# Banded attention: score products in 64x64 quarters of the array, values products in row halves

## The chip, the cores and the metric

One NeuronCore of a Trainium2 chip (trn2). The time is the device time of one launch in microseconds; "span" is the length of the profiled execution, about 1.7 us shorter than the time of the same run. Runs come as fast or slow (slow: over 1.5% above the fastest of the same kernel); fast runs are compared with fast runs.

## The reference

Causal attention with ALiBi bias in a band of 128 keys (8 batches, 8 heads, 576 positions, head width 64), then a token mixer on the 8x576x512 result:

```python
scores = q @ k.T / 8 + slope[h] * -(i - j)          # where 0 <= i - j < 128, else -1e9
x = softmax(scores) @ v                              # heads side by side: [8, 576, 512]
W = (x @ w_q) @ (x @ w_k).T / 8
out = relu(W @ x) @ w_out
```

## The kernel before

Everything is laid out by hand: a list of operations, each with its engine, and one fixed order for each engine. Loads of q, k, v go through one DMA queue; GpSimd casts to fp16; TensorE (PE) transposes q and k; then come scores, exponentials (ScalarE, ACT), multiplication by a table of exp(bias) and mask (VectorE, DVE), values, normalisation, and the mixer. The parts that the change touches:

```python
# scores: key tiles of 128 keys; two heads at once, in the two row halves of the array (64 rows each)
for kb in ((0, 1), (2, 3, 4))[u]:
    for i in range(2):
        ps, r = bank(bk[i]), slice(64 * i, 64 * i + 64)
        ...                                            # a, w: 256, 192 or 64 query columns
        nc.tensor.matmul(ps[:, a : a + w], kk, qT[b % 2][r, c, P * kb : P * kb + w], start=True, stop=True)
nc.scalar.activation(out=pt[:, n % 4, :, 512 * u : 512 * u + 512], in_=..., func=AF.Exp, scale=SCALE)   # 128x1024
nc.vector.tensor_tensor(out=p_, in0=p_, in1=table[:, h0 : h0 + 3 : 2, :], op=ALU.mult)                  # 128x2048

# values: 18 products over all 128 rows for each pair of heads
for t in range(5):
    for i in range(2):
        o = px_of(bk)[:, i, 100 * t : 100 * t + 65]
        ...
        if t > 0:
            nc.tensor.matmul(o, p_[:, a : a + P], vt[b % 2][:, t - 1, hv], start=True, stop=False)
        ...
        nc.tensor.matmul(o, p_[:, a : a + P], vv, start=(t == 0), stop=True)
```

Each `matmul` becomes two PE instructions ("rows" from here on): a weight load and the product (2308 of each in the trace). A "step" below is the work of one pair of heads of one batch, 32 in all. Key tiles of 128 keys against 256 queries compute much that the band masks out; that is what the change goes after.

The softmax here doesn't subtract the row's maximum and nothing guards it: scores larger than these inputs give would overflow.

## Time and profile before

| | before |
|---|---|
| time, median of 3 | 151.97 us (151.51 to 154.68, the last a slow run) |
| span | 149.7 us |
| PE, DVE, ACT busy | 84%, 84%, 79% |
| PE rows in its program | 4618 (2308 weight loads and 2308 products in the trace) |

The waits of the kernel before (who waited for what: us in total, times, longest). "issue" is idle time for which the profile shows no cause:

```profile
PEld L159 <- issue: 21.9, 61, 1.0
...
PE bank L159 <- issue: 1.3, 2, 0.8
```

PEld's "issue" total of 21.9 us did not hold up the products: PE itself waited only 1.3 us for nothing visible.

Busy time by stretches of 30 us (stretch, length, then us busy and instructions of PE, PEld, DVE, ACT and POOL; the last columns are the granted clock, the DMA share and GB/s):

```profile
0.00:30.00 30.00, 20.02 (x392) 16.39 (x393) 23.10 (x43) 23.44 (x31) 11.94 (x20) 1.00 1.03 286
30.00:60.00 30.00, 25.01 (x540) 17.29 (x541) 27.80 (x44) 24.72 (x35) 18.14 (x23) 1.00 1.02 270
60.00:90.00 30.00, 27.94 (x528) 17.70 (x527) 27.67 (x47) 27.39 (x38) 15.67 (x18) 1.00 1.05 332
90.00:120.00 30.00, 28.19 (x526) 17.67 (x528) 28.42 (x46) 26.74 (x42) 12.55 (x18) 1.00 0.93 254
```

PE handles about 530 products in 30 us.

### The profile page before, as it was taken

What the parts mean: (1) busy time and instruction counts of PE and PEld (TensorE: products, weight loads), DVE (VectorE), ACT (ScalarE), POOL (GpSimd) and SP (SyncE); (2) the same over time, 40 slices, a digit from 0 to 9 for tenths busy, and PEclk for the clock granted to TensorE, in tenths of its full rate; (3) what the DMA queues carried; (4) which work ended last, traced back from release to release, by engine and by line L of the source; (5) the groups of instructions that cost most, each with busy time, mean ns of one, the idle gap of its engine ahead of it and who ended that gap; (6) DMA issues with size and microseconds to landing.
All of it is one profiled execution on the core that took longest, in us unless ns stands there. A gap on an engine that the chain in (4) does not pass through costs nothing.

```text
span 149.7 us, 5314 instructions
## 1 busy us (share of the span) xinstructions
PE 125.7 (84%) x2308; PEld 82.6 (55%) x2308; DVE 125.7 (84%) x212; ACT 118.5 (79%) x170; POOL 58.9 (39%) x78
## 2 busy tenths in 40 slices
PE   6567388676889979889989999999789999999870
PEld 6465167555756456547466566576544757555320
DVE  5749987979999998789999989999799989994700
ACT  6959937995889868997799999959889989741560
POOL 4064137354915767333845381364341710000000
PEclk9999999999999999999999999999999999999999
DMA  4999999999999999999999999799699896033075
GB/s 151 383 327 266 180 365 351 264 171 358 389 263 191 296 299 195 236 306 309 348 348 372 338 405 227 167 254 279 157 371 340 235 385 222 4 140 144 0 314 176
DMA packets 50775, 39.40 MB, mean 263 GB/s; under 512 B 39488, under 2 KB 39488, under 8 KB 50752
## 3 DMA queue, kind: packets, MB, share of 16 engines
q1 hardware_dynamic: 50752, 39.07, 88.7%
q8 instruction: 18, 0.29, 0.8%
q14 instruction: 5, 0.04, 0.1%
HBM read 29.62 MB, written 9.44 MB: 261 GB/s over the span
## 4 chain that ended last, share of the span: by engine, by line
PE 40%; DMA 16%; DVE 13%; ACT 12%; SPq 9%; POOL 4%; issue 2%; POOLq 0%; DVEq 0%
PE bank L159 40%; DMA ld<-in_q_dram 10%; SPq L159 9%; ACT pt L159 8%; DMA ld<-in_k_dram 6%; DVE pt L159 5%; POOL nat L159 2%; ACT qT L159 2%; DVE xT L159 2%; POOL vt L159 2%; DVE x L159 2%; ACT kT L159 1%; DVE kT L159 1%; DVE osb L159 1%; DVE rm L159 1%
## 5 line engine op out<-in xcount | busy, mean ns | idle before, releaser
L159 ACT ACTIVATE pt<-bank 128x1024 f16<-128x1024 f32 x64 | 62.7, 1036 | 9.3 <-PE bank L159 9.0
L159 POOL CAST nat<-ld 128x1152 f16<-128x1152 f32 x30 | 34.2, 1146 | 36.7 <-PE bank L159 10.6
L159 DVE TENSOR_TENSOR pt<-pt,table 128x2048 f16<-128x2048 f16 x32 | 41.0, 1293 | 2.1 <-ACT pt L159 2.0
L159 PE MATMUL bank<-wout_sb,rm 128*128 128x512 f16 x128 | 31.8, 380 | 0.0
L159 POOL CAST vt<-ldv 128x512 f16<-128x512 f32 (+1 forms) x35 | 20.8, 613 | 25.4 <-DVE pt L159 15.5
L159 PE MATMUL bank<-qT,kT 64*128 64x256 f16 (+2 forms) x320 | 25.4, 267 | 4.6 <-ACT qT L159 2.0
L159 PE MATMUL bank<-vt,pt 128*128 128x65 f16 x576 | 23.7, 200 | 4.6 <-ACT pt L159 3.1
L159 PEld LDWEIGHTS <-pt 128*128 128x128 f16 x576 | 21.4, 102 | 9.7 <-issue 2.6
L159 DVE TENSOR_TENSOR x<-bank,inv 128x640 f16<-128x640 f32 x32 | 25.8, 817 | 0.8
L159 PEld LDWEIGHTS <-kT 64*128 64x128 f16 x320 | 14.5, 99 | 11.5 <-issue 8.6
L159 ACT COPY osb<-bank 128x512 f32<-128x512 f32 x24 | 13.9, 606 | 7.1 <-PE bank L159 7.1
L159 PE MATMUL bank<-ident,nat 64*128 64x64 f16 x576 | 14.7, 199 | 5.6 <-POOL nat L159 2.8
L159 PEld LDWEIGHTS <-nat 64*128 64x128 f16 x576 | 12.2, 100 | 10.1 <-POOL nat L159 4.7
L159 PEld LDWEIGHTS <-rm 128*128 128x128 f16 x128 | 10.8, 98 | 12.6 <-issue 2.5
L159 ACT COPY qT<-bank 128x1152 f16<-128x1152 f16 x12 | 13.5, 1121 | 2.6 <-PE bank L159 2.6
L159 ACT ACTIVATE rm<-bank 128x512 f16<-128x512 f32 x21 | 12.7, 610 | 2.2 <-PE bank L159 2.2
L159 DVE COPY kT<-bank 128x1152 f16<-128x1152 f16 x8 | 10.8, 1354 | 3.2 <-PE bank L159 3.2
L159 DVE COPY xT<-bank 128x640 f16<-128x640 f16 (+1 forms) x32 | 12.5, 448 | 0.4 <-PE bank L159 0.4
L159 PE MATMUL bank<-x,wkn 128*64 128x512 f16 x80 | 10.1, 383 | 0.0
L159 PE MATMUL bank<-wqT,gm 64*128 64x256 f16 x64 | 8.4, 288 | 1.5 <-DVE wqT L159 0.6
L159 ACT COPY kT<-bank 128x1152 f16<-128x1152 f16 x8 | 9.1, 1138 | 0.5 <-PE bank L159 0.5
L159 DVE TENSOR_SCALAR rm<-bank 128x512 f16<-128x512 f32 x11 | 7.5, 684 | 2.3 <-PE bank L159 2.2
(45 smaller groups left out, 112.1 us busy)
## 6 DMA issues: line engine op xcount, KB each, us to landing
ld<-in_k_dram SPq DMA_DIRECT2D x16, 576.0 KB, 6.9
ld<-in_q_dram SPq DMA_DIRECT2D x16, 576.0 KB, 7.0
ldv<-in_v_dram SPq DMA_DIRECT2D x32, 256.0 KB, 7.1
out_dram<-osb SPq DMA_DIRECT2D x16, 512.0 KB, 5.2
ldv<-in_v_dram SPq DMA_DIRECT2D x8, 128.0 KB, 7.3
osb<-in_moe_w_out_dram SPq DMA_DIRECT2D x2, 512.0 KB, 7.1
out_dram<-osbt SPq DMA_DIRECT2D x8, 128.0 KB, 3.8
osbt<-in_moe_w_q_dram SPq DMA_DIRECT2D x1, 128.0 KB, 5.3
```

What stands on the lines that cost most here:

```text
L159: r = call(*a, **k)
```

## The change

Key tiles of 64 keys need only the two or three query tiles of 64 that the band reaches: 24 tiles of 64 columns for two heads, stacked on the partition halves, instead of 2048 columns for the pair. So the exponentials fall from 64 to 48 and the bias products from 2048 to 1536 columns. Score products shrink to 64x64 quarters, meant to run four at once; values are summed over 64 rows each, two heads at once in the row halves. (One product over 128 rows repeated every 30 ns before.) All operations were put in a new fixed order. The diff, cut to its core (table building, the v loads by pairs of heads, zero pads and the order list are cut):

```diff
-                    for kb in ((0, 1), (2, 3, 4))[u]:
+                    for s, t, n in units[u]:            # 14 (key tile, query tile, count) in three units
                         for i in range(2):
-                            nc.tensor.matmul(ps[:, a : a + w], kk, qT[b % 2][r, c, P * kb : P * kb + w], ...)
+                            for a in range(2):
+                                r, o = slice(64 * i, 64 * i + 64), slice(64 * a, 64 * a + 64)
+                                nc.tensor.matmul(
+                                    bank(bk[i])[o, w : w + 64 * n],
+                                    kT[b % 2][r, 2 * f + a, 64 * s : 64 * s + 64],
+                                    qT[b % 2][r, 2 * f + a, 64 * t : 64 * t + 64 * n],
+                                    start=True, stop=True)
...
-                nc.vector.tensor_tensor(out=p_, in0=p_, in1=table[:, h0 : h0 + 3 : 2, :],
+                    nc.vector.tensor_tensor(out=p_, in0=p_,
+                                            in1=table[:, n].rearrange("p (k w) -> p k w", k=6),
...
-                        (18 products over 128 rows)
+                    terms = [(j, column[j, j])]
+                    if t < 4:
+                        terms += [(j + 1, column[j + 1, j + 1] - 64)]
+                    if t > 0:
+                        terms += [(j - 1, column[j - 1, j]), (j - 2, column[j - 2, j])]
+                    for m, (s, a) in enumerate(terms):                      # 17 terms, 34 products
+                        for i in range(2):
+                            r = slice(64 * i, 64 * i + 64)
+                            nc.tensor.matmul(px_of(bk)[:, i, 100 * t : 100 * t + 65],
+                                             pt[r, c, a : a + P], vt[b % 2][r, s, c],
+                                             start=(m == 0), stop=(m == len(terms) - 1))
```

PE's program grows from 2308 products to 3396.

More of the change, by code (lines that the diff above doesn't have):

```diff
@@ L99 @@
 PLAN = """
-1G 6D 39S 4D 0G 35S 2D 7D 47S 3G 8P0 5D 43S 14P0 20A 65S 19A 11P0 23A 59S 18A 12P0 17A 61S 24A 25D
-21A 9P0 57S 22A 40A 15P0 53S 26D 13P0 51S 10P0 55S 36A 41P2 73S 42D2 69S 37P0 31S 38A0 48G 33S
-250P0 99S 49P2 251A0 44G 245P4 91S 50D2 243P6 77S 244A6 45P0 248P2 66G 46D0 246A4 249A2 67P6 247D
-260P0 255P4 261A0 258P2 62G 68D6 60A 253P0 259A2 58D 63P6 252D 64A6 256A4 262D 254A0 52D 54D 56A
-257D 85S 403P0 95S 406P2 79S 404D0 74G 405D0 265P4 81S 263P6 266A4 407D2 83S 408D2 411P0 70G 87S
@@ L105 @@
-264A6 414P4 412D0 413D0 117S 75P2 32G 71P6 29S 415D4 34G 409P0 416D4 72A6 27S 410D0 113S 417P4
-76A2 268P6 100G 418D4 270P0 269A6 280P2 267D 101P4 281A2 273P6 92G 102D4 274A6 531P2 78G 271A0
-532D2 278P6 93P4 86G 275P2 279A6 272D 535P0 94A4 96G 533P1 536D0 276A2 534D1 80G 537P4 539P0 277D
-111S 97P2 538A4 16P6 125S 98A2 82G 540D0 109S 84G 105S 282D 103S 427P0 419P2 107S 88G 428D0 121S
-295P4 420D2 429D0 422P6 296A4 143S 421D2 293P0 118G 89P4 294A0 423D6 424D6 430P2 90A4 431D2 30G
-541P0 425P6 432D2 542A0 283P4 426D6 433P2 284A4 28G 288P0 434D2 285P6 286A6 297D 290P4 547P2 289A0
@@ L111 @@
-543P6 287D 545P3 544A6 300P0 114G 546D3 291A4 119P6 548D2 549P3 120D6 301A0 126G 298P4 550A3 115P0
-292D 127P6 299A4 650P2 110G 128D6 116A0 645P3 106G 651A2 112G 137S 557P0 646D3 553P4 104G 643P2
-139S 554A4 558D0 133S 108G 644A2 135S 302D 435P0 131S 438P2 129S 122G 436D0 310P4 439D2 440D2
-648P6 147S 311A4 647S 437D0 303P2 144G 649A6 123P4 304A2 124D4 138G 145P0 446P6 146A0 308P2 140G
-447D6 448D6 443P4 309A2 555P0 444D4 441P6 134G 445D4 556A0 141P2 142A2 442D6 449P0 305P4 136G
-450D0 306A4 551P6 313P2 552D6 559P0 314A2 132G 307D 315P4 163S 318P6 316A4 320P2 157S 655P1 130G
@@ L117 @@
-560D0 151S 319A6 451P4 159S 321A2 663P0 148G 195S 452D4 453D4 177S 323P6 664A0 312D 325P2 165S
-149P4 656A1 161S 563P0 324A6 322D 169S 326A2 561P1 155S 317D 652S 454P6 564A0 462P2 150A4 164G
-455D6 562D1 653P0 463D2 152G 456D6 459P4 654A0 464D2 660P1 160G 657S 460D4 158G 461D4 173S 153P2
-661A1 328P6 189S 154D2 658P0 329A6 196G 203S 330P4 191S 659D0 565P6 333P2 331A4 199S 566D6 178G
-457P0 334A2 465P4 458D0 197P6 466D4 198A6 338P0 166G 571P2 572D2 340P4 339A0 573P6 327D 341A4
-575P7 162G 574D6 335P0 569P2 567P4 336A0 170G 577P6 568D4 570A2 576D7 156G 179P0 578D6 167P2 180A0
@@ L123 @@
-171P4 332D 467P6 168A2 666P0 337D 172A4 668P1 468D6 469D6 470P2 667A0 669A1 579P4 471D2 581P6
-472D2 174G 580A4 673P0 670S 582A6 662S 585P2 342D 175P4 185S 586A2 345P6 671P1 346A6 183S 190G
-674D0 181S 478P2 204G 176A4 672D1 187S 348P6 479D2 207S 480D2 475P0 349A6 192G 350P4 476D0 583P2
-477D0 351A4 473P6 200G 474D6 481P0 584A2 343P4 482D0 344A4 353P6 355P2 352D 587P0 356A2 683P1
-588D0 354A6 347D 678P0 684A1 186G 193P2 679A0 358P4 194D2 360P6 359A4 591P0 184G 361A6 357D 215S
-201P2 205P4 209S 202A2 589P1 182G 592D0 221S 681P6 590D1 206A4 217S 188G 211S 362D 491P0 682A6
@@ L129 @@
-233S 483P2 225S 492D0 486P4 484D2 216G 493D0 676P6 208G 487D4 485D2 686P7 210G 677A6 488D4 680S
-597P0 687A7 370P2 598D0 213S 494P4 371A2 222G 675S 593P6 495D4 373P0 594A6 496D4 241S 489P2 374A0
-229S 380P6 490D2 218G 497P4 665S 498D4 381A6 223P2 375P0 212G 224D2 365P4 237S 376A0 601P6 235S
-366A4 603P7 602D6 685S 377D 363P0 239S 599P2 368P4 364A0 605P6 600D2 226G 369A4 604D7 595P0 606D6
-234G 227P2 596A0 219P4 372D 378P6 220A4 696P0 214G 228D2 379A6 694P1 697A0 367D 613P4 607P2 609P6
-608A2 689P0 610A6 382D 507P2 614A4 691P6 690A0 242G 508D2 509D2 695A1 499P4 230G 692A6 611P0 500D4
@@ L135 @@
-383P2 501D4 612A0 693S 502P6 384A2 688S 238G 231P0 503D6 504D6 510P4 232A0 698S 709P2 236G 511D4
-512D4 385P0 505P6 386A0 400P4 506D6 701P3 401A4 710D2 240G 398P0 702D3 513P6 711S 399A0 393P4
-514D6 699P2 394A4 402D 615P3 700A2 395P0 616D3 388P4 703S 396A0 390P6 387D 617P2 389A4 619P3 618D2
-397D 391A6 515P0 706P2 620A3 516D0 392D 621P4 625P6 622A4 704P3 517D0 707A2 626D6 518P4 705A3
-627P0 519D4 708S 523P6 520D4 628A0 623P2 524D6 526P0 624A2 525D6 521P4 527D0 528D0 714P2 522D4
-529P0 715A2 712P3 530D0 629P2 713D3 631P0 630D2 716S 633P1 632D0 717P0 634A1 639P2 637P4 635P6
@@ L141 @@
-640A2 638D4 641P2 636D6 719P1 642A2 718D0 727P2 720D1 729P3 728A2 721S 724P2 730A3 731S 722P3
-725A2 732P2 723A3 726S 733A2 734S
+0G 6D 34S 30S 4D 1G 11P0 54S 2D 12P0 42S 14P0 5D 38S 3G 7P0 58S 46S 13P0 19A 9P0 18A 35G 17A 48S
+21D 8P0 16A 15P0 50S 36P2 31A 20D 10P0 52S 37A2 32P0 55G 62S 33A0 66S 56P2 78S 222P0 43G 57D2
+226P4 28S 223A0 224P6 26S 225A6 44P2 82S 39G 45D2 70S 227A4 40P0 59G 41A0 72S 228D 76S 230P0 234P2
+231A0 232P4 229D 60P6 74S 235A2 47G 61D6 22S 49G 350P0 233A4 24S 353P2 351D0 51G 86S 238P4 236D
@@ new lines @@
+240P6 90S 239A4 102S 53G 354D2 352D0 242P4 106S 237D 243A4 96S 358P0 63G 355D2 241A6 94S 359D0
+356P2 360D0 64P4 361P6 67G 100S 65A4 357D2 362D6 68P0 363D6 98S 79G 69A0 364P2 114S 365D2 29G 80P0
+110S 27G 250P4 81A0 245D 248P6 126S 478P2 244D 249A6 246P0 480P3 83G 479D2 251A4 482P2 481D3 247A0
+71G 84P4 483A2 253D 366P0 85A4 486P2 484P6 73G 367D0 368D0 485A6 120S 369P4 77G 487A2 490P0 370D4
+256P6 491A0 371D4 130S 377P2 257A6 488P0 252D 372P4 489A0 75G 373D4 254P6 258P0 255A6 23G 378D2
+379D2 374P4 259A0 375D4 25G 376D4 380P0 260D 597P2 87G 381D0 590P3 598A2 88P0 91G 591D3 492P2 89A0
@@ new lines @@
+493D2 92P4 261D 592P0 93A4 103G 593D0 262P2 266P4 263A2 594S 107G 494P0 138S 104P6 267A4 495D0 97G
+134S 264P2 105D6 108P0 118S 265A2 595P4 95G 109A0 124S 385P2 268D 382P6 596A4 150S 101G 386D2
+274P0 383D6 387D2 496P4 122S 275A0 384D6 99G 154S 272P2 497A4 270P0 269D 599S 273A2 390P6 142S
+500P4 391D6 115G 501A4 392D6 393P2 271A0 504P4 394D2 502P6 395D2 505A4 111G 498P0 503D6 388P2
+499A0 116P4 276D 112P6 117A4 610P0 127G 389D2 113A6 600P1 277D 611A0 396P2 601A1 282P4 121G 397D2
+280P6 283A4 128P0 131G 278P2 129D0 281A6 506P4 602P5 279A2 507D4 607P4 603A5 139G 604S 401P0 608A4
@@ new lines @@
+158S 132P2 402D0 285D 140P4 133A2 144S 508P6 135G 403D0 510P7 141A4 148S 509D6 119G 136P0 511D7
+162S 398P2 137A0 284D 146S 288P4 290P6 125G 399D2 289A4 605P0 400D2 174S 291A6 178S 512P4 151G
+409P2 168S 513D4 606A0 518P6 410D2 519A6 152P4 411D2 166S 404P0 123G 153A4 516P6 405D0 406P2 182S
+517A6 407D2 286P4 155G 186S 408D2 514P0 287A4 296P6 609S 515D0 412P2 170S 297A6 298P4 293D 294P0
+299A4 172S 292D 615P6 295A0 613P7 143G 413D2 198S 301D 520P0 614A7 618P1 616A6 300D 617S 156P2
+521D0 159G 202S 522P4 157A2 619D1 190S 524P5 523D4 145G 160P0 525D5 192S 417P2 161A0 414P6 149G
@@ new lines @@
+418D2 306P4 415D6 416D6 620P0 307A4 419D2 163G 528P6 425P4 529A6 621D0 164P2 426D4 622S 147G 427D4
+304P0 165A2 206S 422P6 210S 305A0 530P2 423D6 175G 302P4 196S 424D6 531A2 532P0 303A4 420P6 533D0
+194S 176P2 179G 421D6 177A2 428P0 526P4 429D0 310P6 527A4 169G 312P2 314P0 311A6 309D 534P4 313A2
+633P5 167G 535D4 308D 315A0 433P6 180P2 634A5 316D 430P0 181A2 538P4 434D6 431D0 432D0 187G 320P2
+435D6 322P0 321A2 183G 536P5 539D4 188P6 323A0 537D5 184P2 189D6 625P4 185A2 171G 317D 540P0 626A4
+436P6 546P2 541A0 438P4 173G 437D6 547A2 544P0 439D4 441P6 440D4 545A0 318P2 199G 442D6 330P0
@@ new lines @@
+443D6 319A2 623P4 331A0 325D 200P2 444P6 624A4 630P5 324D 627S 628P4 203G 445D6 631A5 216S 201A2
+548P5 629D4 191G 612S 326P0 549D5 204P2 327A0 328P4 205D2 214S 193G 446P6 329A4 449P0 632S 447D6
+448D6 542P2 218S 550P4 543A2 332D 552P5 220S 551D4 207G 450D0 336P2 553D5 636P4 635S 337A2 451D0
+211G 554P6 637A4 558P2 560P0 555D6 559A2 638P5 333D 561A0 212P2 639A5 208P6 197G 213A2 338P0 209D6
+640S 457P4 195G 339A0 334P2 458D4 459D4 452P6 335A2 454P0 453D6 344P4 342P2 455D0 345A4 456D0
+641P6 217G 343A2 341D 556P0 346P4 557A0 643P7 340D 347A4 460P0 215G 465P2 642A6 461D0 462P4 466D2
@@ L143 @@
+348D 648P6 463D4 349D 646P0 649A6 644A7 562P1 219G 464D4 647A0 645S 656P6 467D2 221G 650S 563D1
+470P4 657A6 468P0 471D4 658S 473P2 469D0 564P6 474D2 475D2 566P7 472D4 651P0 567A7 565D6 568P2
+476P4 569A2 574P6 477D4 653P1 575A6 652D0 576P2 654A1 570P4 577D2 655S 572P0 571A4 578P3 573D0
+580P2 579D3 659P3 581A2 584P0 660A3 661P2 585D0 582P4 662A2 586P0 588P6 587A0 664P3 589D6 663S
+583D4 666P2 665D3 679P0 667D2 671P1 680A0 668S 669P0 681S 672A1 674P1 670A0 673S 676P0 675A1 677A0
+678S
 """
-RINGS = {"ld": 8, "ldv": 8, "nat": 6, "vt": 10, "qT": 4, "kT": 4, "P": 4, "x": 8, "xT": 8,
+RINGS = {"ld": 8, "ldv": 8, "nat": 6, "vt": 8, "qT": 4, "kT": 4, "P": 4, "x": 8, "xT": 8,
@@ L253, in steps @@
     ld = [sb([P, 2, 576], FP32, f"ld{i}") for i in range(RINGS["ld"])]
-    ldv = [sb([P, H, D], FP32, f"ldv{i}") for i in range(RINGS["ldv"])]
+    ldv = [sb([P, S], FP32, f"ldv{i}") for i in range(RINGS["ldv"])]
     nat = [sb([P, 9, 2, D], F16, f"nat{i}") for i in range(RINGS["nat"])]
-    vt = [sb([P, 5, 520], F16, f"vt{i}") for i in range(2)]
+    vt = [sb([P, 9, 4, 65], F16, f"vt{i}") for i in range(2)]
     qT = [sb([P, 4, S], F16, f"qT{i}") for i in range(2)]
-    kT = [sb([P, 4, 640], F16, f"kT{i}") for i in range(2)]
-    pt = sb([P, 4, 2, 1088], F16, "pt")
-    table = sb([P, H, 1024], F16, "table")
+    kT = [sb([P, 4, S], F16, f"kT{i}") for i in range(2)]
+    pt = sb([P, 4, 1984], F16, "pt")
+    table = sb([P, 4, 1536], F16, "table")
+    slope = sb([P, 4], FP32, "slope")
+    exps = sb([P, 4, 192], F16, "exps")
     xs = [sb([P, 5, DM], F16, f"x{i}") for i in range(2)]
@@ L274, in steps @@
     wout_sb = sb([P, 4, DM], F16, "wout_sb")
-    rel = sb([P, 256], FP32, "rel")
-    reli = sb([P, 256], I32, "reli")
+    rel = sb([P, 192], FP32, "rel")
+    reli = sb([P, 192], I32, "reli")
     inv = [sb([P, 2, 5], FP32, f"inv{i}") for i in range(3)]
@@ L299, in f_iota @@
     def f_iota(eng, bk):
-        nc.gpsimd.iota(reli, pattern=[[1, 256]], base=0, channel_multiplier=-1)
+        for i in range(2):
+            nc.gpsimd.iota(reli[64 * i : 64 * i + 64], pattern=[[1, 192]], base=0,
+                           channel_multiplier=-1)
     def f_rel(eng, bk):
         copy(eng, rel, reli)
+        for n in range(4):
+            for i in range(2):
+                nc.vector.memset(slope[64 * i : 64 * i + 64, n : n + 1],
+                                 -(2.0 ** (-(2 * n + i + 1))))
     def f_mask(eng, bk):
-        nc.gpsimd.affine_select(out=rel, in_=rel, compare_op=ALU.is_ge, fill=1.0e9, base=0,
-                                pattern=[[1, 256]], channel_multiplier=-1)
-        nc.gpsimd.affine_select(out=rel, in_=rel, compare_op=ALU.is_ge, fill=1.0e9, base=127,
-                                pattern=[[-1, 256]], channel_multiplier=1)
+        for i in range(2):
+            r = rel[64 * i : 64 * i + 64]
+            nc.gpsimd.affine_select(out=r, in_=r, compare_op=ALU.is_ge, fill=1.0e9, base=0,
+                                    pattern=[[1, 192]], channel_multiplier=-1)
+            nc.gpsimd.affine_select(out=r, in_=r, compare_op=ALU.is_ge, fill=1.0e9, base=127,
+                                    pattern=[[-1, 192]], channel_multiplier=1)
     def f_zero(eng, bk):
@@ L316, in f_ones @@
         for i in range(2):
-            nc.vector.memset(vt[i][:, :, 64:520:65], 1.0)
-            nc.vector.memset(vt[i][64:128, 4], 0.0)
-    def f_kzero(eng, bk):
-        for i in range(2):
-            nc.vector.memset(kT[i][:, :, S:640], 0.0)
+            nc.vector.memset(vt[i][:, :, :, 64], 1.0)
     def f_pads(eng, bk):
-        nc.vector.memset(pt[:, :, :, 1024:1088], 1.0)
+        nc.vector.memset(pt[:, :, 0:1920].rearrange("p n (k w) -> p n k w", k=6)[:, :, :, 0:64],
+                         0.0)
+        nc.vector.memset(pt[:, :, 1920:1984], 0.0)
     op({"POOL": 0.9}, "ident", -99, f_ident, writes=[("ident", 0)])
-    op({"POOL": 0.35}, "iota", -98, f_iota, writes=[("iota", 0)])
-    op({"DVE": 0.35}, "rel", -97, f_rel, reads=[("iota", 0)], writes=[("rel", 0)])
-    op({"POOL": 0.8}, "mask", -96, f_mask, reads=[("rel", 0)], writes=[("mask", 0)])
-    op({"DVE": 0.5}, "k zero", -98, f_kzero, writes=[("kzero", 0)])
-    op({"DVE": 0.5}, "ones", -15, f_ones, writes=[("ones", 0)])
+    op({"POOL": 0.6}, "iota", -98, f_iota, writes=[("iota", 0)])
+    op({"DVE": 0.8}, "rel", -97, f_rel, reads=[("iota", 0)], writes=[("rel", 0)])
+    op({"POOL": 1.4}, "mask", -96, f_mask, reads=[("rel", 0)], writes=[("mask", 0)])
+    op({"DVE": 0.2}, "ones", -15, f_ones, writes=[("ones", 0)])
     op({"DVE": 0.3}, "zero", -14, f_zero, writes=[("zero", 0)])
-    op({"DVE": 0.45}, "pads", -10, f_pads, writes=[("pads", 0)])
+    op({"DVE": 0.7}, "pads", -10, f_pads, writes=[("pads", 0)])
     for i in range(9):
@@ L341, in steps, with f_exps, put @@
            opens=(f"warm{i}", 1))
-    for h in range(H):
-        def f_exps(eng, bk, h=h):
-            nc.scalar.activation(out=table[:, h, 0:256], in_=rel, func=AF.Exp,
-                                 scale=-(2.0 ** (-(h + 1))))
-        op({"ACT": 0.29}, f"exps{h}", -30 + h, f_exps, reads=[("mask", 0)], writes=[("exps", h)])
+    for n in range(4):
+        def f_exps(eng, bk, n=n):
+            nc.scalar.activation(out=exps[:, n], in_=rel, func=AF.Exp, scale=slope[:, n : n + 1])
+        op({"ACT": 0.34}, f"exps{n}", -30 + n, f_exps, reads=[("mask", 0), ("rel", 0)],
+           writes=[("exps", n)])
     for f in range(2):
         def f_table(eng, bk, f=f):
-            t = table[:, 4 * f : 4 * f + 4]
-            for a in range(1, 4):
-                w = 256 if a < 3 else 192
-                nc.vector.tensor_copy(out=t[:, :, 256 * a : 256 * a + w], in_=t[:, :, 0:w])
-            nc.vector.tensor_copy(out=t[:, :, 960:1024], in_=t[:, :, 0:64])
-        op({"DVE": 1.15}, f"table{f}", -20 + 2 * f * SLOT, f_table,
-           reads=[("exps", 4 * f + h) for h in range(4)], writes=[("table", f)])
+            e, t = exps[:, 2 * f : 2 * f + 2], table[:, 2 * f : 2 * f + 2]
+            def put(first, piece, count=1):
+                w = piece.shape[-1]
+                if count > 1:
+                    nc.vector.tensor_copy(
+                        out=t[:, :, first : first + count * w].rearrange("p n (k w) -> p n k w",
+                                                                         k=count),
+                        in_=piece.unsqueeze(2).broadcast_to([P, 2, count, w]))
+                else:
+                    nc.vector.tensor_copy(out=t[:, :, first : first + w], in_=piece)
+            put(0, e[:, :, 0:128], 2)
+            put(256, e[:, :, 0:64])
+            put(320, e)
+            put(512, e[:, :, 0:64])
+            put(576, e[:, :, 0:128])
+            put(704, e[:, :, 64:128])
+            for k in range(3):
+                put(768 + 256 * k, e)
+                put(960 + 256 * k, e[:, :, 128:192])
+        op({"DVE": 1.6}, f"table{f}", -20 + 2 * f * SLOT, f_table,
+           reads=[("exps", 2 * f + n) for n in range(2)], writes=[("table", f)])
     def f_ldw(eng, bk, i):
@@ L420, in steps @@
                 op({"ACT": 1.0, "DVE": 1.26}, "evac " + name, base - 3.5,
-                   f_evac, psum=key, reads=[("kzero", 0)] * x, writes=[(("qT", "kT")[x], 2 * b + f)])
-        for kb in range(5):
-            i = 5 * b + kb
+                   f_evac, psum=key, writes=[(("qT", "kT")[x], 2 * b + f)])
+        for n in range(4):
+            i = 4 * b + n
             t = ldv[i % RINGS["ldv"]]
-            w = P if kb < 4 else TAIL
-            def f_loadv(eng, bk, b=b, kb=kb, t=t, w=w):
-                nc.sync.dma_start(out=t[0:w], in_=v[b, :, P * kb : P * kb + w, :].rearrange(
-                    "h s d -> s h d"))
-            def f_castv(eng, bk, b=b, kb=kb, t=t, w=w):
-                copy(eng, vt[b % 2][0:w, kb, :].rearrange("p (h e) -> p h e", h=H)[:, :, 0:D],
-                     t[0:w])
-            base = b * PERIOD + 0.5 * kb
-            op({"SP": 0.6}, f"ld v{b}{kb}", base - 12, f_loadv, writes=[("ldv", i)],
-               dma=1.33 if kb < 4 else 0.67)
-            op({"POOL": 0.6} if b else {"POOL": 0.6, "DVE": 0.6, "ACT": 0.5}, f"cast v{b}{kb}",
-               base - 5, f_castv, reads=[("ldv", i), ("ones", 0)], writes=[("vt", i)])
@@ L441, in steps @@
-    for b in range(NB):
-        for c in range(4):
-            base, n = b * PERIOD + c * SLOT, 4 * b + c
-            for u in range(2):
-                def f_scores(eng, bk, b=b, c=c, u=u):
-                    for kb in ((0, 1), (2, 3, 4))[u]:
-                        for i in range(2):
-                            ps, r = bank(bk[i]), slice(64 * i, 64 * i + 64)
-                            a = 256 * (kb - 2 * u) if kb < 4 else 448
-                            if kb < 4:
-                                kk = kT[b % 2][r, c, P * kb : P * kb + P]
-                                w = 256 if kb < 3 else 192
-                            else:
-                                kk, w = kT[b % 2][r, c, 512:640], 64
-                            nc.tensor.matmul(ps[:, a : a + w], kk,
-                                             qT[b % 2][r, c, P * kb : P * kb + w],
-                                             start=True, stop=True)
-                def f_exp(eng, bk, n=n, u=u):
-                    nc.scalar.activation(
-                        out=pt[:, n % 4, :, 512 * u : 512 * u + 512],
-                        in_=pairs[bk[0] // 2].rearrange("p (i r) -> p i r", i=2), func=AF.Exp,
-                        scale=SCALE)
-                key = f"S{b}{c}{u}"
-                op({"PE": 0.24}, key, base + 0.95 * u - 0.8, f_scores,
-                   reads=[("qT", 2 * b + c // 2), ("kT", 2 * b + c // 2)],
-                   opens=(key, 2), mode="R")
-                op({"ACT": 0.93}, f"E{b}{c}{u}", base + 0.95 * u - 0.5, f_exp, psum=key,
-                   reads=[("pads", 0)], writes=[("P", n)])
-            def f_bias(eng, bk, n=n, h0=4 * (c // 2) + c % 2):
-                p_ = pt[:, n % 4, :, 0:1024]
-                nc.vector.tensor_tensor(out=p_, in0=p_, in1=table[:, h0 : h0 + 3 : 2, :],
-                                        op=ALU.mult)
-            h0 = 4 * (c // 2) + c % 2
-            op({"DVE": 1.15}, f"M{b}{c}", base + 1.5, f_bias,
-               reads=[("P", n), ("table", c // 2)], writes=[("PM", n)])
@@ new lines, in f_loadv, with f_castv @@
+            def f_loadv(eng, bk, b=b, n=n, t=t):
+                for a in range(2):
+                    nc.sync.dma_start(
+                        out=t[64 * a : 64 * a + 64].rearrange("p (s d) -> p s d", d=D),
+                        in_=v[b, 2 * n + a].rearrange("(s p) d -> p s d", p=64))
+            def f_castv(eng, bk, b=b, n=n, t=t):
+                copy(eng, vt[b % 2][:, :, n, 0:D], t.rearrange("p (s d) -> p s d", d=D))
+            base = b * PERIOD + n * SLOT
+            op({"SP": 1.15}, f"ld v{b}{n}", base - 12, f_loadv, writes=[("ldv", i)], dma=1.5)
@@ new lines, in steps @@
+            op({"POOL": 0.65} if b else {"POOL": 0.65, "DVE": 0.65, "ACT": 0.55}, f"cast v{b}{n}",
+               base - 5, f_castv, reads=[("ldv", i), ("ones", 0)], writes=[("vt", i)])
+    units = (((4, 4, 2), (6, 6, 2), (7, 7, 1), (2, 2, 2), (6, 8, 1)),
+             ((8, 8, 1), (0, 0, 2), (7, 8, 1), (1, 1, 3), (0, 2, 1)),
+             ((3, 3, 3), (2, 4, 1), (5, 5, 3), (4, 6, 1)))
+    column = {}
+    for u in range(3):
+        w = 0
+        for s, t, n in units[u]:
+            for j in range(n):
+                column[s, t + j] = 320 * (2 * u + w // 256) + 64 + w % 256
+                w += 64
@@ new lines, in steps, with f_scores, f_exp, f_bias @@
+    for b in range(NB):
+        for f in range(2):
+            base = b * PERIOD + 2 * f * SLOT
+            for u in range(3):
+                def f_scores(eng, bk, b=b, f=f, u=u):
+                    w = 0
+                    for s, t, n in units[u]:
+                        for i in range(2):
+                            for a in range(2):
+                                r, o = slice(64 * i, 64 * i + 64), slice(64 * a, 64 * a + 64)
[4 more added lines that the diff above has]
+                                    start=True, stop=True)
+                        w += 64 * n
+                def f_exp(eng, bk, f=f, u=u):
+                    p_ = pt[:, 2 * f : 2 * f + 2, 0:1920].rearrange("p i (k w) -> p i k w", k=6)
+                    nc.scalar.activation(
+                        out=p_[:, :, 2 * u : 2 * u + 2, 64:320],
+                        in_=pairs[bk[0] // 2].rearrange("p (i k w) -> p i k w", i=2, k=2),
+                        func=AF.Exp, scale=SCALE)
+                key = f"S{b}{f}{u}"
+                op({"PE": 0.26}, key, base + 1.9 * u - 0.8, f_scores,
+                   reads=[("qT", 2 * b + f), ("kT", 2 * b + f)], opens=(key, 2), mode="Q")
+                op({"ACT": 0.93}, f"E{b}{f}{u}", base + 1.9 * u - 0.5, f_exp, psum=key,
+                   reads=[("pads", 0)], writes=[("P", 4 * b + 2 * f), ("P", 4 * b + 2 * f + 1)])
+            for n in range(2 * f, 2 * f + 2):
+                def f_bias(eng, bk, n=n):
+                    p_ = pt[:, n, 0:1920].rearrange("p (k w) -> p k w", k=6)[:, :, 64:320]
+                    nc.vector.tensor_tensor(out=p_, in0=p_,
+                                            in1=table[:, n].rearrange("p (k w) -> p k w", k=6),
+                                            op=ALU.mult)
+                op({"DVE": 0.9}, f"M{b}{n}", base + 1.5, f_bias,
+                   reads=[("P", 4 * b + n), ("table", f)], writes=[("PM", 4 * b + n)])
@@ L482, in steps, with f_values @@
             n, prio = 4 * b + c, b * PERIOD + (c + 1) * SLOT
-            h0 = 4 * (c // 2) + c % 2
             def px_of(bk):
                 return pairs[bk[0] // 2].rearrange("p (i r) -> p i r", i=2)
-            def f_values(eng, bk, b=b, n=n, h0=h0):
+            def f_values(eng, bk, b=b, c=c):
                 for t in range(5):
-                    for i in range(2):
-                        o = px_of(bk)[:, i, 100 * t : 100 * t + 65]
-                        hv = slice(65 * (h0 + 2 * i), 65 * (h0 + 2 * i) + 65)
-                        p_ = pt[:, n % 4, i]
-                        if t > 0:
-                            a = 256 * t - 128
-                            nc.tensor.matmul(o, p_[:, a : a + P], vt[b % 2][:, t - 1, hv],
-                                             start=True, stop=False)
-                        a = 256 * t if t < 4 else 960
-                        vv = vt[b % 2][:, t, hv]
-                        nc.tensor.matmul(o, p_[:, a : a + P], vv, start=(t == 0), stop=True)
+                    j = 2 * t
+                    terms = [(j, column[j, j])]
[4 more added lines that the diff above has]
+                    for m, (s, a) in enumerate(terms):
+                        for i in range(2):
+                            r = slice(64 * i, 64 * i + 64)
+                            nc.tensor.matmul(px_of(bk)[:, i, 100 * t : 100 * t + 65],
+                                             pt[r, c, a : a + P], vt[b % 2][r, s, c],
+                                             start=(m == 0), stop=(m == len(terms) - 1))
             def f_recip(eng, bk, n=n):
@@ L504, in f_recip, with f_norm @@
                 nc.vector.reciprocal(out=inv[n % 3], in_=px[:, :, :, 64])
-            def f_norm(eng, bk, b=b, n=n, h0=h0):
+            def f_norm(eng, bk, b=b, c=c, n=n):
                 px = px_of(bk)[:, :, 0:500].rearrange("p i (t w) -> p i t w", t=5)
                 nc.vector.tensor_tensor(
-                    out=xs[b % 2].rearrange("p t (h d) -> p h t d", h=H)[:, h0 : h0 + 3 : 2],
+                    out=xs[b % 2].rearrange("p t (h d) -> p h t d", h=H)[:, 2 * c : 2 * c + 2],
                     in0=px[:, :, :, 0:64],
@@ L512, in steps @@
             key = f"PV{b}{c}"
-            op({"PE": 0.54}, key, prio, f_values,
-               reads=[("P", n), ("PM", n)] + [("vt", 5 * b + t) for t in range(5)], opens=(key, 2))
+            op({"PE": 0.52}, key, prio, f_values,
+               reads=[("P", n), ("PM", n), ("vt", n)], opens=(key, 2), mode="R")
             op({"DVE": 0.1}, f"NR{b}{c}", prio + 0.5, f_recip, psum=key, writes=[("inv", n)],
```

## The prediction

> **What bounds it now.** The page: span 149.7 us, PE and DVE busy 84%, ACT 79%. Two things bind in turn. (1) DMA: the queue table gives 88.7% of 16 engines' span, 132.8 us; by stretches its share is 0.92 to 1.11 up to 120 us. Landings fit a queue that never runs dry: 1.81 us per load of q or k, about 1.3 per store and per 128 keys of v, summed in issue order, put the last k load at 116.2 us; the trace has 116.3. (2) Then PE: the last k transposes start at 118.07 us, and the timeline shows PE without a gap from there to 145.06 us, as the chain of waits does. DVE is close behind: 13.4 to 14.4 us busy of every 15 from 45 to 135 us.
>
> **The change, costed from the trace.**
> - ACT: 64 exponentials of 128x1024 become 48, at 1.036 us: -16.6 us. Table building -2, more evacuations +6: 118.5 to about 107.
> - DVE: 32 bias products shrink from 2048 to 1536 columns, 1.293 to about 0.95 us: -11. With evacuations moved to ACT and more table copies: 125.7 to about 110.
> - PE scores: a unit of 512 columns takes about 225 ns (pairs of 256 columns repeat every 109 ns). 64 units become 48, each again 512 columns, in short quarters. If four run at once, 0.26 us each: 14.4 to 12.5. [...]
> - PE values: 18 products over 128 rows (29.5 ns apart, 0.545 us) become 34 in row halves. Transposes already run as 64-row pairs, 29 ns per pair: 17 pairs are 0.51 us. -1 us in all.
> - Mode switches: [...] 126 ns from a values to a score product instead of 30, about 95 ns each. PE's order has 95 before, 108 after: +1.2 us.
> - PE in sum: 111.6 to about 110 us of pure work, hardly changed, with 1088 more products.
> - DMA: same bytes, same 256-byte packets for v: unchanged, 132 us.
>
> **On the critical path.** ACT and DVE relief is mostly off it; it buys slack, so that PE follows its data more closely. What counts is the new order: the last q and k loads stand before six v loads and behind fewer stores, so a full queue lands them at about 110 us instead of 116. From the last transposes on PE has 27.3 us of work (25.2 before). 110 + 1.5 (cast, wait) + 27.3 + 4.3 (evacuation, store) gives 143 us if PE has caught up; if it is as late in its list as before (72 us of work done at 105 us) it reaches those transposes at 115.5 and ends at 147. Timed runs are about 2 us over the span. I predict 146.5 us, range 142 to 151; faster by over 2% 0.70, within 2% 0.22, slower 0.08.
>
> **Signs.** Exponentials 48 at 1.0 us; bias products 0.9 to 1.0; ACT and DVE under 78% busy; DMA share near 1 to 115 us; values pairs and 64-column score quads 29 ns apart; last q or k landing near 110 us; PE unbroken from about 113.
>
> **What would make it wrong.** Quarters that don't run four at once or wait for weights [...]; dearer switches; loads issued late because their buffers are held, so that the DMA queue runs dry; a startup lengthened by the table's many copies.

Where the text is marked as cut, it said of the array what no run or trace of this case shows, or guessed from that: what short quads might cost, and a range for it among the risks. 110 + 1.5 + 27.3 + 4.3 = 143 us of span, or 147 if PE is as late as before, and about 2 us more for a timed run; predicted were 146.5 us. In PE's sum the 95 ns of a mode switch are measured (126 ns less 30), and 13 more of them are its +1.2 us.

## More of the kernel before

Lines of the page of the kernel before: busy time of each engine with instruction counts; granted PE clock and DMA share in 40 slices (9 is 90% or more); the DMA queues (packets, megabytes, share of 16 engines); groups of instructions (line, engine, operation, shapes, count, then busy us, mean ns, idle time ahead of them).

```profile
span 149.7 us, 5314 instructions
...
PE 125.7 (84%) x2308; PEld 82.6 (55%) x2308; DVE 125.7 (84%) x212; ACT 118.5 (79%) x170; POOL 58.9 (39%) x78
...
PEclk9999999999999999999999999999999999999999
DMA  4999999999999999999999999799699896033075
...
q1 hardware_dynamic: 50752, 39.07, 88.7%
q8 instruction: 18, 0.29, 0.8%
...
L159 ACT ACTIVATE pt<-bank 128x1024 f16<-128x1024 f32 x64 | 62.7, 1036 | 9.3 <-PE bank L159 9.0
...
L159 DVE TENSOR_TENSOR pt<-pt,table 128x2048 f16<-128x2048 f16 x32 | 41.0, 1293 | 2.1 <-ACT pt L159 2.0
...
L159 PE MATMUL bank<-qT,kT 64*128 64x256 f16 (+2 forms) x320 | 25.4, 267 | 4.6 <-ACT qT L159 2.0
L159 PE MATMUL bank<-vt,pt 128*128 128x65 f16 x576 | 23.7, 200 | 4.6 <-ACT pt L159 3.1
```

Three engines are close together, the DMA engines look full until slice 30 (112 us), and the clock line shows 9 in all 40 slices. One line seems to be mere bookkeeping and turns out to be the one that counts: the queue `q8 instruction`, 18 packets and 0.29 MB, so 16 KB each. I read it as PE's own program, because its packets follow PE's rows, one for each 256: 18 for 4618 here, 26 for 6794 in the kernel after, 22 for about 5770 in a kernel of the experiments (row halves, cut loads).

## The result, and the profile after

| | before | after |
|---|---|---|
| time, median of 4 runs each | 152.61 us (151.51 to 154.68) | 172.94 us (172.52 to 173.78) |
| span | 149.7 us | 170.8 us |
| ratio of fast runs | | 1.137 (95%: 1.126 to 1.147) |

A ratio is the mean time of one kernel's fast runs over that of the other's of the same rounds, so not quite the ratio of the medians (154.68 is a slow run and left out of it). The change made the kernel 13.7% slower; 146.5 us was predicted.

The same lines of the page, after:

```profile
span 170.8 us, 7562 instructions
...
PE 131.5 (77%) x3396; PEld 88.0 (52%) x3396; DVE 112.6 (66%) x221; ACT 108.1 (63%) x156; POOL 60.7 (36%) x79
...
PEclk9999978697856999579999999969999999999999
DMA  5999999899989999973999999999618880163265
...
q1 hardware_dynamic: 51136, 39.07, 83.2%
q8 instruction: 26, 0.43, 1.2%
...
L156 ACT ACTIVATE pt<-bank 128x1024 f16<-128x1024 f32 x48 | 46.9, 1032 | 16.2 <-PE bank L156 16.1
...
L156 PE MATMUL bank<-vt,pt 64*128 64x65 f16 x1088 | 25.5, 202 | 11.9 <-issue 10.4
...
L156 DVE TENSOR_TENSOR pt<-pt,table 128x1536 f16<-128x1536 f16 x32 | 30.2, 962 | 1.0 <-ACT pt L156 1.0
...
L156 PE MATMUL bank<-qT,kT 64*64 64x64 f16 (+2 forms) x896 | 20.2, 230 | 7.3 <-issue 5.1
```

ACT and DVE fell as intended, and now idle. No engine is over 77% busy. Two things are new: idle time ahead of values and scores with the releaser "issue", and a granted clock that falls to half.

The waits after:

```profile
PEld L156 <- issue: 43.5, 68, 3.7
...
PE bank L156 <- issue: 21.5, 13, 3.6
```

PE waits 21.5 us, up to 3.6 us at a time, for nothing that the profile shows. The timeline of PE around one such wait (start, length, what, count, idle time ahead of it):

```profile
43.13 0.95 PE L156 MATMUL bank<-vt,pt 64*128 64x65 f16 x28
47.48 0.35 PE L156 MATMUL bank<-vt,pt 64*128 64x65 f16 x6 [3.39 <-issue]
49.00 0.71 PE L156 MATMUL bank<-ident,x 64*128 64x64 f16 x18 [1.17 <-DVE x L156]
49.65 3.60 PE L156 MATMUL bank<-wout_sb,rm 128*128 128x512 f16 x8
```

PE stops in the middle of one step, between two values products whose operands have long been ready, and no semaphore is involved. Afterwards eight output products take 3.60 us: PE runs at half clock (the clock's records give 0.5 from 47.45 us on, for 6.83 us). The timeline of the kernel before has such eight in 1.90 us:

```profile
48.29 1.90 PE L159 MATMUL bank<-wout_sb,rm 128*128 128x512 f16 x8
```

The stretches after:

```profile
0.00:30.00 30.00, 17.65 (x511) 15.72 (x511) 18.99 (x56) 16.91 (x19) 15.16 (x26) 0.94 0.98 266
30.00:60.00 30.00, 22.24 (x556) 14.84 (x549) 17.51 (x29) 18.13 (x25) 11.41 (x13) 0.77 1.00 280
60.00:90.00 30.00, 25.38 (x748) 16.75 (x751) 20.97 (x39) 22.88 (x34) 12.77 (x14) 0.89 0.92 228
90.00:120.00 30.00, 23.38 (x677) 15.95 (x677) 21.07 (x37) 20.33 (x27) 11.09 (x13) 0.94 1.06 280
```

**Where the stops are.** I numbered PE's rows (weight loads, products and the few semaphore instructions, 9 in the kernel after) in the order of the trace and looked for rows that wait for no semaphore and yet start over 0.25 us after the row ahead of them. In the kernel after, 13 such stops, 24.3 us in all, stand at row 193 of a block of 256 rows: 449, 705, 961, 1473, 1729, 2241, 2497, 3521, 3777, 4545, 5057, 5569, 6081. In the kernel before there are two, of 0.72 and 1.02 us. A packet of the instruction queue has 16,384 bytes by its record; at one packet for 256 rows that makes 64 bytes for each. Put beside the packets of that queue (times in us):

```
row    fetch packet from  to      row starts   after the packet's end   gap ahead of the row
 705   20.65              21.59   22.97        1.37                     2.74
 961   26.36              27.92   29.44        1.52                     3.11
1729   44.66              45.99   47.48        1.48                     3.63
2497   64.64              66.17   67.45        1.28                     2.20
4545   109.03             109.99  111.43       1.44                     3.77
```

At all 13 stops PE goes on 1.26 to 1.52 us after its packet ended. I read that as PE having run out of instructions; the experiments below test it. Packets start between 0 and 4.8 us after PE passes row 193 of the block ahead, in both kernels. So each block seems to be asked for one block ahead (this is read off the times, not shown by a record), and takes the delay, 0.9 to 1.8 us of packet, and about 1.4 us more: some 2.6 to 7.3 us. PE passes values products in row halves at one pair, four rows, in 30 ns, so it can pass 256 rows in 1.9 us. With the stops left out, a block of 256 rows took PE 5.1 us at least in the kernel before (median 7.1), and 2.4 us at least in the kernel after (median 4.6). The fetches did not get later: their median delay was 2.93 us before and 1.77 us after. The rows got faster.

**The clock.** Six periods of half clock, 27.3 us in all, begin at 23.56, 30.39, 40.63, 47.45, 67.93 and 112.30 us: each within 1 us of the end of a stop of 1.5 us or more (22.97, 29.44, 40.18, 47.48, 67.45, 111.43). One of 1.84 us, at 123.34, was followed by none. The six beginnings lie whole multiples of 3.413 us apart, and in the 3.41 us ahead of each PE idled for 1.9 to 3.4 us. The stop of 1.84 us fell across a border of this grid (122.54 us), with 1.0 us of idling ahead of it. No sharp limit comes out of this: a stretch of the kernel after with 1.9 us of idling (from 13.3 us) and one of the kernel before with 2.1 us (from 17.3 us) were not followed by half clock. The periods are 3.41 us long or twice that (6.83 us), and 1.9 us of idling in the stretch ahead was the least that one of them followed. 483 products ran in these periods; against the median of the same product at full clock they took some 8.5 us longer.

24.26 - 1.74 = 22.5 us more of stops and 8.5 us of half clock are 31 us; the span grew by 21.1. The rest, 10 us, would by this sum be what lighter ACT and DVE gave back, but the sum is not shown. The other three timed runs of the changed kernel had a granted clock of 0.841, 0.850 and 0.861, against 0.919 in the profiled one, which makes 1.7 to 2 times its half clock, and took 173.78, 172.52 and 173.33 us against 172.55. So much more half clock went with 1.2 us more at most, and its 8.5 us can't simply be added to the stops.

### The profile page after: what moved, and what is told of

Same layout as the page of the kernel before. It is cut to its first block, busy times and chain, and to the rows that moved or that the text cites. A ratio compares the mean times of both kernels' runs of the same rounds, so it can differ in the third digit from the quotient of the medians.

```text
span 170.8 us, 7562 instructions
## 1 busy us (share of the span) xinstructions
PE 131.5 (77%) x3396; PEld 88.0 (52%) x3396; DVE 112.6 (66%) x221; ACT 108.1 (63%) x156; POOL 60.7 (36%) x79
## 3 DMA queue, kind: packets, MB, share of 16 engines
q1 hardware_dynamic: 51136, 39.07, 83.2%
## 4 chain that ended last, share of the span: by engine, by line
PE 42%; issue 18%; ACT 14%; DMA 12%; DVE 7%; POOL 4%; POOLq 0%; ACTq 0%
PE bank L156 42%; ACT pt L156 6%; DMA ld<-in_k_dram 5%; DMA ldv<-in_v_dram 4%; DVE table L156 4%; ACT qT L156 3%; ACT osb L156 2%; DMA out_dram<-osb 2%; POOL vt L156 2%; ACT kT L156 1%; POOL wout_sb L156 1%; ACT rm L156 1%; DVE kT L156 1%; ACT L156 1%; POOL nat L156 1%
## 5 line engine op out<-in xcount | busy, mean ns | idle before, releaser
L156 ACT ACTIVATE pt<-bank 128x1024 f16<-128x1024 f32 x48 | 46.9, 1032 | 16.2 <-PE bank L156 16.1
L156 PE MATMUL bank<-vt,pt 64*128 64x65 f16 x1088 | 25.5, 202 | 11.9 <-issue 10.4
L156 POOL CAST vt<-ldv 128x576 f16<-128x576 f32 x32 | 21.1, 676 | 35.0 <-DVE pt L156 19.6
L156 DVE TENSOR_TENSOR pt<-pt,table 128x1536 f16<-128x1536 f16 x32 | 30.2, 962 | 1.0 <-ACT pt L156 1.0
L156 PEld LDWEIGHTS <-pt 64*128 64x128 f16 x1088 | 22.1, 102 | 16.3 <-issue 12.9
L156 PE MATMUL bank<-qT,kT 64*64 64x64 f16 (+2 forms) x896 | 20.2, 230 | 7.3 <-issue 5.1
L156 PEld LDWEIGHTS <-kT 64*64 64x64 f16 x896 | 15.2, 118 | 11.6 <-issue 7.6
L156 ACT COPY kT<-bank 128x1152 f16<-128x1152 f16 x12 | 13.4, 1127 | 6.6 <-PE bank L156 6.6
L156 PE MATMUL bank<-ident,x 64*128 64x64 f16 x288 | 8.9, 206 | 3.5 <-DVE x L156 2.5
L156 PE MATMUL bank<-wqT,gm 64*128 64x256 f16 (+1 forms) x64 | 9.5, 297 | 2.0 <-issue 1.5
L156 PEld LDWEIGHTS <-x 64*128 64x128 f16 x288 | 7.3, 105 | 6.1 <-issue 3.6
```

The lines of the kernel that those rows point to most:

```text
L156: r = call(*a, **k)
```

## The experiments

Theory A: PE waits for its program, because rows pass faster than blocks arrive, and blocks are delayed behind data packets. Theory B: quarters or row halves are slow in themselves, or counted as idle by the clock. Theory C: the new order is bad. "Stops" below are those at row 193 of a block, without a semaphore, over 0.25 us.

### Row halves alone, in the kernel before

```diff
+                    terms = [x for x in terms for _ in range(2)]
+                    for m, (a, s) in enumerate(terms):
+                        for i in range(2):
+                            r = slice(64 * i, 64 * i + 64)
...
+                            nc.tensor.matmul(px_of(bk)[:, i, 100 * t : 100 * t + 65],
+                                             pt[r, n % 4, i, a : a + P], vt[b % 2][r, s, hv],
+                                             start=(m == 0), stop=(m == len(terms) - 1))
```

Each head uses one half twice, so that the result is wrong.

> The kernel before, only its 18 values products per step over 128 rows replaced by 36 in row halves, two at once (each half twice, so that the result is wrong on purpose; score table flattened to keep it finite). Same array time (18 pairs of 29 ns for 18 of 29.5 ns), no quarters, same plan, ACT, DVE and DMA; PE rows rise from 4618 to about 5770. Theory A (PE waits for its instructions: blocks of 256 rows, each asked for only one block ahead and delayed behind data packets): slower by 3 to 8%, stalls without a semaphore at rows 193 modulo 256 that sum to 5 to 15 us (before: about 2), and half clock after the long ones. Theory B (quarters of the array are at fault: slow, or counted as idle by the clock): same within 1.5%, stalls about 2 us, clock full.

Measured: one fast run of 157.40 us (three more, 163.66 to 165.51 us, count as slow) against fast runs of before of 150.14 to 151.92. The three slow runs had no clearly lower clock (0.892 to 0.952 against 0.938), so what made them slower stays open; the loss is 4% by the one fast run. That run was the profiled one: five stops, 7.7 us; half clock 17.1 us. Its timeline shows a stop in the middle of transposes, work that the kernel before does in the same way:

```profile
43.42 0.22 PE L159 MATMUL bank<-ident,x 64*128 64x64 f16 x3
46.38 0.38 PE L159 MATMUL bank<-ident,x 64*128 64x64 f16 x14 [2.75 <-issue]
```

So 1152 more rows bring the stops without any quarter and in the old order. That is against C, and against quarters as the cause; a half-clock period from 17 to 24 us had no stop ahead of it, so row halves as such were not cleared by this run. (A later profile of the kernel before, with cut loads, had half clock from 7.8 to 24.9 us with no stop and no row halves; so the early clock differs between profiles without either.)

### Fewer rows for more array time

```diff
-                    for j in range(9):
-                        for a in range(2):
-                            r = slice(64 * a, 64 * a + 64)
-                            o = bank(bk[a]).bitcast(F16)
-                            nc.tensor.transpose(o[:, 64 * j : 64 * j + 64], n[r, j]..., ident[r, r])
+                    o = pairs[bk[0] // 2].bitcast(F16)
+                    for j in range(9):
+                        nc.tensor.transpose(o[:, P * j : P * j + P], n[:, j]..., ident)
```

> The changed kernel, the 18 half transposes of q and k (64 rows, pairs of 29 ns) replaced by 9 full ones of 128 columns (about 55 ns): 576 PE rows fewer (two and a quarter blocks of 256), but about 0.24 us more array time per step, 7.6 us in all. Correct result. Theory A: 2 to 6% faster than the changed kernel (ratio to before 1.07 to 1.12), because rows and not array time bind. Theory B or any theory in which PE's array time binds: slower than the changed kernel, ratio 1.15 to 1.19.

Measured: ratio 1.138 (1.129 to 1.146): neither. Stops fell from 24.3 to 16.9 us (8 instead of 13), and the added array time took that back. Its 7.6 us are an estimate from the trace of the kernel before: a product of 512 columns repeats every 216 ns, so one of 128 columns was put at about 55 ns, and nine of them replace nine pairs of 29 ns, 0.24 us a step in 32 steps. My expectation had weighed only one side. As the profile shows both, it speaks for A's mechanism, but the time alone tells nothing.

> The control of the run above: the same full transposes in the kernel before. Both theories: not faster than before; array time binds there in the last third, so 1 to 5% slower, stalls at block boundaries under 2 us.

Measured: ratio 1.022 (1.016 to 1.028), no stop at all. In the kernel before, some 3.3 of the estimated 7.6 us of extra array time show in the total.

### DMA traffic away

From the third batch on, loads of q, k and v fetch one partition only (in the kernel before, and with row halves, v is cut only from the second tile of the fourth batch on, so the whole run moves 19.4 MB of data instead of 18.1); casts read stale data, so the result is wrong. Rows, array work, order and stores stay.

```diff
+                    w = P if b < 2 else 1
-                    nc.sync.dma_start(out=t, in_=srcs[x][b].rearrange(...)[f])
+                    nc.sync.dma_start(out=t[0:w], in_=srcs[x][b].rearrange(...)[f][0:w])
```

> The changed kernel with the loads of q, k and v cut to one partition each from the third batch on (stale data, wrong on purpose; stores unchanged), so that the DMA engines are mostly idle after the first 30 us. Theory A: the fetch of a block starts about 1 us after it is asked for instead of 1 to 4.7, the stalls at block boundaries fall from 25 us to 5 to 12 us, half clock nearly gone, span 125 to 145 us. Theory B: stalls or slow quarters stay as they are, and with them the half clock; span above 150 us.

Measured in one look: 149.56 us, span 147.8, just above A's 125 to 145; six stops, 6.8 us (2.3 us of it after 30 us).

> The control of the run with cut loads: the kernel before with the same cut (wrong on purpose). Says how much of the 170.8 to 147.8 us that the changed kernel gained is only the data arriving sooner. If instruction blocks are what separates the two kernels (theory A), the changed one, now with 6.8 us of stalls, should be close: this one at 138 to 148 us, within 10 us of it, against 21 us with full loads. If the new order or the quarters themselves are bad (theory C), the distance stays near 20 us: this one under 131 us.

Measured in one look: 148.39 us, span 146.7, no stop. The distance of 21 us was gone. Both were repeated in rounds on one chip, with the row-half kernel as a third:

> The kernel before with values in row halves (the first experiment, 163.8 us against 150.3) and the loads cut from the third batch on; wrong on purpose. Theory A (fetch of PE rows delayed behind data): the loss of 13 us goes with the data traffic: 147 to 153 us, within 4 us of the kernel before with cut loads, stalls after 30 us under 2 us. If row halves cost time by themselves (array, clock): still 10 us or more above the kernel before with cut loads.

> The changed kernel with cut loads again, timed in rounds this time. Theory A: as in the one look, 146 to 153 us. If that look was chance: over 158 us.

> The kernel before with cut loads again, timed in rounds: 146 to 150 us, so that the three kernels with cut loads lie within 5 us of each other on one chip.

(The 163.8 us in the first of these texts is the median with the slow runs; the fast one was 157.4.)

| kernel | full loads | cut loads | stops, full | stops, cut |
|---|---|---|---|---|
| before | 150.95 us (1) | 148.92 us, ratio 0.986 (0.976 to 0.995) | 1.7 us | 0 |
| before with row halves | 157.40 us (one fast run) | 151.71 us, ratio 1.004 (0.994 to 1.014) | 7.7 us | 2.5 us |
| after | 172.94 us (2) | 146.64 us, ratio 0.970 (0.961 to 0.979) | 24.3 us | 4.2 us |

Medians; ratios to the kernel before with full loads in the same rounds; (1) is its median there, with the stops of its first profile; (2) the result above, from other rounds, as is the 157.40. Lines of the pages of two of them, the kernel after with cut loads first, then the row-half kernel with cut loads:

```profile
span 144.8 us, 7562 instructions
...
PE 122.4 (85%) x3396; PEld 82.5 (57%) x3396; DVE 112.4 (78%) x221; ACT 106.7 (74%) x156; POOL 60.9 (42%) x79
...
PEclk9999999779999999999999999999999999999997
DMA  4999999880001203030031330000542501803384
```

```profile
span 150.4 us, 6466 instructions
...
PEclk9999999999999999999999999999999999999999
DMA  4999999740950006003300070004540465033075
```

With the same program and the same order, the changed kernel sheds 26 us when most load packets go, 20.1 us of stops among them, and the kernel before sheds 2. The changed kernel is then the faster one (0.970 against 0.986). The fetch packet starts a median of 0.97 us after row 193 passes instead of 1.77 (in the kernel before 0.80 instead of 2.93), and the clock of the changed kernel stays full but for one period of 3.4 us. C falls: the order by itself costs nothing (whether another order would stop less under full loads was not tried). B falls: quarters and row halves run at full clock in nearly all of the last two pages, and the row-half kernel is 2.8 us (1.9%) above the kernel before with cut loads, 2.5 us of which are stops. The three lie 5.1 us apart. The pair also shows that the kernel before was hardly bound by its loads after the first batches: without them it gains 1.5%. Stores stayed.

### A shorter DMA queue

```diff
+        if o.name.startswith("ld "):
+            if len(loads) >= 3:
+                for w in loads[-3].insts:
+                    tc.add_manual_dep(o.insts[0], w.name, ...)      # wait until that load has landed
+            loads.append(o)
```

> The changed kernel, each load issued only when the load three before it has landed, so that less data stands in the DMA engines ahead of a fetch. Correct result, same rows, same array work. Theory A: fetches start sooner (median delay under 1.7 us, none over 3.5), stalls 10 to 20 us instead of 25, 2 to 6% faster than the changed kernel (ratio to before 1.07 to 1.12) unless the DMA queue runs dry. Theory of DMA bandwidth or of quarters: no gain or slower, ratio 1.13 to 1.18.

> As above with two loads in flight. Theory A: median delay under 1.4 us and stalls under 12 us; but two loads in flight no longer fill the queue (first load 3.8 us alone for 0.59 MB), so the total may be anywhere from 1.05 to 1.15. Otherwise: 1.15 to 1.25, with stalls unchanged.

> The control of the limit of three: in the kernel before, which has under 2 us of stalls, it can only cost data. Both theories: 0 to 5% slower than before.

| | ratio to before | stops |
|---|---|---|
| after, three loads in flight | 1.112 (1.102 to 1.122) | 14.7 us (profile of a slow run) |
| after, two | 1.240 (1.232 to 1.249) | 0.5 us |
| before, three | 1.067 (1.056 to 1.078) | 0 |

The limit of three costs the kernel before 6.7%, more than the 5% expected, and still seems to help the kernel after (1.137 without it, in other rounds on another chip; the intervals nearly touch). The median delay of the fetch did not fall (1.80 us), only its longest (4.0), so that part of the expectation failed. With two, stops nearly vanish, median delay 1.31 us, but the total misses A's range, because data comes too late: the waits name the landing of v (32.1 us) and of k (24.0 us) as what GpSimd waits for. The stops follow the queue of data, but holding data back is no cure.

### Rows alone, by extra weight loads: failed

```diff
+                            for _ in range(2):
+                                nc.tensor.ldweights(p_[:, a : a + P])
                             nc.tensor.matmul(o, p_[:, a : a + P], ...)
```

> The kernel before with two more weight loads of the same weights ahead of each values product: 1152 PE rows more (5770), no product, no mode, no array half more; result correct. [...] Theory A: slower by 4 to 10%, stalls without a semaphore at rows 193 modulo 256 of 5 to 15 us, half clock after the long ones. Theory B (row halves or quarters as such): under 1.5% plus what the array time shows, stalls under 2.5 us, clock full.

> The same 1152 rows more, but put where PE passes rows slowly: eight more weight loads ahead of each product of the output stage, which takes 216 ns each. Result correct. Theory A: far less harm than the run above, because a block of 256 rows is asked for about 256 rows ahead and these rows lie where time is plenty, yet they take away slow stretches elsewhere: 1 to 5% slower, stalls 2 to 8 us. If the mere count of rows decides: the same loss as the run above.

> The first run of this set with the loads cut from the third batch on (wrong on purpose), to be set against the kernel before with cut loads (148.39 us). Theory A: with the DMA engines idle the same 1152 rows cost little: 148 to 153 us, stalls after 30 us under 2 us. If the extra weight loads cost array time: the same loss as with full loads.

The cut in the first text is a guess at the time of a weight load that no trace had shown.

Measured: ratio 1.284 and, at the output products, 1.136, both far above A's ranges, but without its stops (0, and one of 0.64 us). With cut loads the first of them still took 193.1 us. In the first, the cost lies in the values steps: at full clock, one takes 1650 ns from its first to its last product instead of 527, (1650 - 527) / 36 = 31 ns for each extra load. It also ran 58 us at half clock, and with cut loads 55 us, without a single stop at row 193: half clock also comes without them. So these runs don't isolate rows. They do show that count alone is not the cause: 5770 rows that pass slowly give no stops, the 5770 rows of the row-half kernel did.

### Fewer values products

```diff
+                    terms = terms[: (len(terms) + 1) // 2]
```

> The changed kernel with only 18 of the 34 values products of a step (wrong on purpose; score table flattened to keep it finite): 1024 PE rows fewer (5770), array time less by 8 pairs of 29 ns in 32 steps, 7.4 us. Theory A: stalls 8 to 15 us instead of 25, faster than the changed kernel by more than the array time: 12 to 22 us, ratio to before 0.99 to 1.06. If array time alone counts: 7 us, ratio 1.08 to 1.10.

Measured: fast runs 159.99 and 161.87 us, ratio 1.064 (1.048 to 1.080), a little outside A's range; the interval ends where the range for array time alone begins. Stops 13.4 us (profile of a slow run) instead of 24.3. About two thirds of the gain over the changed kernel (7.4 of some 11 us) would be array time by the estimate.

## Why the prediction was wrong

- **The step that failed** is "PE in sum: 111.6 to about 110 us of pure work, hardly changed, with 1088 more products". The array time was about right, but the products' instructions were taken as free. They were fetched in 26 packets instead of 18, and while data filled the DMA engines, rows in row halves and quarters passed faster (256 of them in 2.4 us at the least) than blocks came (2.6 to 7.3 us). The missing term measured 22.5 us of stops. Half clock came in their wake, but what it cost stays open. The fetch of instructions does not stand under "What would make it wrong" either; the page's line of the instruction queue was there to be read.
- **"DMA: ... unchanged"** was right of the data (39.07 MB in both) and left out that PE's program comes by DMA too (queue q8, 0.43 MB), and that its packets started later with the data packets there (a median of 1.77 us against 0.97 with cut loads).
- **"Two things bind in turn. (1) DMA"** was wrong, at least after the first two batches. The queue looked full and landing times fitted a full queue, but with loads cut the kernel before gained only 1.5%. Here the full queue showed that loads were issued early, not that anybody waited for them.
- **The order.** "a full queue lands them at about 110 us": the last q and k landed at 117.7 and 120.6 us, because they were issued only at 112.8 and 113.3 us. They stand in one queue behind stores and earlier loads, and up to then the queue had waited 10.2 us for results to store (two waits, 3.7 and 6.5 us) and 4.9 us for GpSimd to free load buffers. PE was unbroken only from 142.8 us, not from 113.
- **Right:** exponentials 48 at 1.032 us; bias products 0.962 us; ACT 108.1 us (107 predicted), DVE 112.6 (110); values pairs 30 ns apart (29). Score quads of 64, 128 and 192 columns repeat every 29, 59 and 86 ns (medians), so the wait of quarters for weights that I had feared did not show. That there is something to gain was right too: with most load packets away the changed kernel is 1.6% faster than the kernel before (0.970 over 0.986). That doesn't confirm the way that was predicted, q and k landing earlier; which part gives the 1.6% was not tested.
- **Open:** when exactly a block is asked for; how far the delay of a fetch depends on bytes ahead of it (the limit of three loads did not lower its median); and the split between stops and clock, which was summed from the trace, not tested apart, and which the clocks of the other timed runs speak against. No version was found that beats the kernel before.

## What to carry to other kernels

Count instructions as well as array time: when a change cuts PE work into smaller tiles, compare how fast 256 rows pass with the 2.6 to 7.3 us that a block of them took to arrive here under full DMA traffic. Idle PE time called "issue" in the middle of a step, at multiples of 256 rows from each other, went from 24.3 to 4.2 us here with cut loads, so I read it as the program arriving late; cut the loads as a test and see whether it goes. And a full DMA queue was no proof that data binds (the kernel before gained 1.5% when its loads were cut): the same test tells.
